# Scores of two heads per matmul: 64x64 array tiles in place of 32x64 ones in a gated mix of linear and sliding-window attention

## The chip, the cores and the metric

The kernel runs on one core of a Trainium2 chip. The metric is the device time of one execution in microseconds. Each kernel is run several times; the median is given. One execution is also profiled.

## The reference

Two attention blocks read the same input x (1 x 2048 x 1024, bf16) and a per-row gate mixes them. Block A is linear attention, block B attends to eight earlier positions at distances 0, 2, ..., 14. Both have 32 heads of 32.

```python
g = sigmoid((x * gate_w).sum(-1, keepdims=True))
return g * A(x, A_wqkv, A_wo) + (1 - g) * B(x, B_wqkv, B_wo)

# A:  pq, pk = phi(q), phi(k);  kv = pk^T v;  z = pk.sum(s)
#     o = (pq @ kv) / (pq . z + 1e-6);  o @ wo
# B:  idx = pos[:, None] - 2 * arange(8)[None, :]          # masked where idx < 0
#     logits = einsum(q[s], k[idx[s, w]]) * 32 ** -0.5
#     o = softmax(logits) @ v[idx];  o @ wo
```

## The kernel before

Rows of x are split by parity into two halves of 1024, so that a window of distance 2 becomes eight neighbouring rows within a half. x is loaded transposed, and the kernel computes V of block B (written to HBM), then K and Q of block B for the first half, then for the second half, then phi(K) of block A, then a matrix mT = xn^T phi(K) and from it the state kv (`state`, L1607), and at last queries, folds and outputs. All these are groups of eight or sixteen matmuls on the full 128x128 array with 512 columns (L1349, L1628, L1700), each into one bank of PSUM; while the windows of block B are worked on, these groups have banks 0 to 3 (0 to 2 later) and the windows have banks 4 to 7 (`SO`).

The windows of block B are done in eighteen *fills*, nine for each half, which are slipped in between those groups (`slot`, one fill in about five groups). Here they are numbered 0 to 17. A fill serves 2 x 57 query rows (2 x 56 in the last of a half), for all heads: two sets of 57 queries, each with its 64 keys. One fill is these steps:

- two DMAs bring the 2 x 64 rows of V back from HBM (tile `v`).
- the **scores burst** (`s_fn`, L1448): for 8 chunks c of four heads, 2 sets h and 4 heads j of a chunk, a matmul of 32 rows (one head's dimensions) by 64 columns (keys) with 57 moving columns (queries). The tile of the array is (32 j, 64 h), so that the eight tiles of a chunk can work at once. Head j of a chunk goes to bank 4 + j.
- ScalarE takes the exponentials of all four banks at once (L1454) into `E`, one of two buffers.
- VectorE multiplies them with the mask (L1457).
- three slots later, the **values burst** (`each`, L1468, 64 matmuls of 64 rows by 32 columns) and within it the sums of the exponentials (L1474, eight matmuls of 456 columns against ones), into the same four banks.
- ScalarE takes the reciprocal of the sums by Ln and Exp (L1483, L1484), VectorE multiplies and writes the result over the queries in `qT` (L1485). After the second of these the banks are free for the next scores burst.

GpSimd makes the masks at the start, and late in the kernel adds up z, the sum of phi(K) over the rows (L1588, L1590; sixteen steps, three after each fill's mask). The cast of z (`zb`, L1570) stands in VectorE's queue between the mask of fill 16 and its L1485.

The order on each engine is not written out: `Prog.schedule` plans it from costs given with each operation and from priorities, in several passes, and the instructions are then emitted per engine in that order, with semaphore waits where data or buffers demand it. An engine works its queue in order.

Of the kernel before, what the change touches and what calls it, by code (L numbers as in the profile page):

```python
# [7 lines left out]
ALU = mybir.AluOpType  # L8
AX = mybir.AxisListType
BF16 = mybir.dt.bfloat16  # L10
# [1109 lines left out]
def build_kernel(nc, A_x, A_wqkv, A_wo, B_x, B_wqkv, B_wo, gate_w, out):  # L1120
# [3 lines left out]
    HS = S // 2  # L1124
# [86 lines left out]
    zb = SB([128, 1024], BF16, "zb")  # L1211
    denr = Ring([SB([128, H], F32, "den%d" % i) for i in range(2)])
    mx4 = SB([128, 3], F32, "mx4")
    mx1 = SB([1, 3], F32, "mx1")
    flag = SB([1, 1], I32, "flag")
    zs = SB([128, 16], F32, "zs")
# [41 lines left out]
    def plan(seen):  # L1258
# [26 lines left out]
            return P.op(eng, fn, cost, reads=reads, writes=writes, prio=-1)  # L1285

        C("pool", lambda e: e.memset(ones[:], 1.0), 0.1, [ones.all()])
        for i, (n, offs) in enumerate(KINDS):
            for h, o in enumerate(offs):
                m = mtmp[h]  # L1290
                b0 = o + 64 * h
                C("pool", lambda e, m=m: e.memset(m[:], 1.0), 0.1, [m.all()])

                C("pool", lambda e, m=m, n=n, b0=b0: e.affine_select(out=m[:, :, 0:n], in_=m[:, :, 0:n], compare_op=ALU.is_ge, fill=0.0, base=b0,
                                                                     pattern=[[0, 2], [1, n]], channel_multiplier=-1), 0.3, [m.all()], [m.all()])
                C("pool", lambda e, m=m, n=n, b0=b0: e.affine_select(out=m[:, :, 0:n], in_=m[:, :, 0:n], compare_op=ALU.is_ge, fill=0.0, base=7 - b0,
                                                                     pattern=[[0, 2], [-1, n]], channel_multiplier=1), 0.3, [m.all()], [m.all()])
                C("dve", lambda e, m=m, n=n, h=h, i=i: e.tensor_copy(msk[i][64 * h:64 * h + 64, :, :], m[64 * h:64 * h + 64, :, 0:n]), 0.2, [msk[i].all()], [m.all()])
                P.ops[-1].prio = 1100
# [132 lines left out]
        masks = []  # L1432
        slot_n = [0]

        def fill(e_, qs, nq, offs):
            t0 = e_ * HS
            k0 = [qs + nq * h - offs[h] for h in range(2)]
# [2 lines left out]
            for h in range(2):  # L1440
                P.op("sp", lambda e, h=h: e.dma_start(vt[64 * h:64 * h + 64, :], vB_hbm[t0 + k0[h]:t0 + k0[h] + 64, :]), 0.4,
                     reads=[hb(t0 + k0[h], t0 + k0[h] + 64, i) for i in range(2)], writes=[vt.all()], chan="v%d_%d" % (vslot, h), lat=0.5)

            def s_fn(e):
                for c in range(8):
                    for h in range(2):
                        for j in range(4):
                            last = e.matmul(SO[j].ap(c * nq, (c + 1) * nq)[64 * h:64 * h + 64, :], kT[32 * j:32 * j + 32, c, t0 + k0[h]:t0 + k0[h] + 64],  # L1448
                                            qT[32 * j:32 * j + 32, c, t0 + qs + h * nq:t0 + qs + (h + 1) * nq], start=True, stop=True, tile_position=(32 * j, 64 * h))
                return last  # L1450
            P.op("pe", s_fn, 0.65, mode="r", reads=[kT.part((0, 8), (t0 + k0[0], t0 + k0[1] + 64)), qT.part((0, 8), (t0 + qs, t0 + qs + 2 * nq))],
                 writes=[s.iv for s in SO], name="S")
            E, _ = Er.next()
            P.op("act", lambda e: e.activation(E[:, 0:32 * nq].rearrange("p (j q) -> p j q", j=4), ps[:, 4:8, 0:8 * nq], ACT.Exp), act(32 * nq),  # L1454
                 reads=[s.iv for s in SO], writes=[E.all()])
# [5 lines left out]
            def values():  # L1461

                def each(e):
                    for c in range(8):
                        for j in range(4):
                            for h in range(2):
                                hd = 4 * c + j
                                last = e.matmul(SO[h].ap(c * nq, (c + 1) * nq)[32 * j:32 * j + 32, :], vt[64 * h:64 * h + 64, hd * 32:hd * 32 + 32],  # L1468
                                         E[64 * h:64 * h + 64, (8 * j + c) * nq:(8 * j + c + 1) * nq],
                                         start=True, stop=True, tile_position=(64 * h, 32 * j))  # L1470
                        if c == SUMS_AT:
                            for j in range(4):
                                for h in range(2):
                                    e.matmul(SO[2 + h].ap(0, 8 * nq)[32 * j:32 * j + 32, :], ones[64 * h:64 * h + 64, 0:32],  # L1474
                                             E[64 * h:64 * h + 64, 8 * j * nq:8 * (j + 1) * nq],
                                             start=True, stop=True, tile_position=(64 * h, 32 * j))
                    return last
                bi = [s.iv for s in SO]
# [347 lines left out]
```

## Time and profile before

| | us |
|---|---|
| median of 3 runs (lowest to highest) | 485.57 (485.45 to 485.61) |
| the profiled execution | 485.35 |
| its span, first to last instruction | 483.5 |
| TensorE busy | 480.0 |
| VectorE, ScalarE, GpSimd busy | 294.9, 146.9, 39.4 |
| granted TensorE clock (share of full) | 1.00 |

In the lines of the profile, PE is TensorE's matmuls and PEld its weight loads, DVE is VectorE, ACT ScalarE, POOL GpSimd. A line of a timeline has the start in us, the length in us, the engine, the line of the kernel, the operation, what it writes and reads, the shapes and the count; merged lines run from the first start to the last end. In brackets stands the idle time before and what ended it. The end of a matmul is modelled: matmuls overlap, so the distance from start to start tells more than the length.

### The profile page before, as it was taken

The numbers are of one execution on the slowest core, as the hardware profiler recorded it, in microseconds if no ns is written. First come the engines' busy times: TensorE is split into PE (matmuls) and PEld (weight loads), VectorE is DVE, ScalarE is ACT, GpSimd is POOL, SyncE is SP. The second block draws the span as 40 slices with busy tenths as digits, with TensorE's granted clock in tenths as the row PEclk, the third lists the DMA queues.
The fourth block names the chain that finished last, engine by engine and source line by source line (L and its number), as shares of the span: only waits on it lengthen the run. The fifth ranks groups of instructions, "written<-read, shape, count | busy, mean of one in ns | idle before, by whom it ended". The sixth has DMA issues, their size and how long they took to land.

```text
span 483.5 us, 10963 instructions
## 1 busy us (share of the span) xinstructions
PE 480.0 (99%) x4882; PEld 229.0 (47%) x4882; DVE 294.9 (61%) x490; ACT 146.9 (30%) x229; POOL 39.4 (8%) x40
## 2 busy tenths in 40 slices
PE   9999999999999999999999999999999999999997
PEld 6444444444444444444455555444444444444444
DVE  2212186799777778766733222489987777767522
ACT  2111111112344446666654356264222000011000
POOL 3000000000000000000015757010000000000000
DMA  8999996223100032013004340571234111122111
GB/s 243 203 190 322 340 342 188 81 94 107 26 23 26 25 110 73 27 34 111 24 25 122 129 104 4 132 197 24 65 89 87 45 43 45 44 66 66 45 45 48
DMA packets 73977, 48.51 MB, mean 100 GB/s; under 512 B 38337, under 2 KB 67394, under 8 KB 73922
## 3 DMA queue, kind: packets, MB, share of 16 engines
q1 hardware_dynamic: 73090, 46.94, 35.5%
q10 hardware_dynamic: 832, 0.79, 0.8%
q8 instruction: 40, 0.66, 0.6%
q14 instruction: 15, 0.12, 0.1%
HBM read 30.41 MB, written 8.39 MB: 80 GB/s over the span
## 4 chain that ended last, share of the span: by engine, by line
PE 99%; DVE 0%; issue 0%
PE ps_all L1349 58%; PE ps_all L1700 23%; PE ps_all L1628 12%; PE ps_all L1448 2%; PE ps_all L1468 2%; PE ps_all L1385 1%; PE ps_all L1474 1%; PE ps_all L1607 1%; PE ps_all L1655 0%; DVE o L1379 0%
## 5 line engine op out<-in xcount | busy, mean ns | idle before, releaser
L1349 PE MATMUL ps_all<-w,xT 128*128 128x512 bf16 x512 | 112.9, 379 | 0.0
L1349 PE MATMUL ps_all<-xT,w 128*128 128x512 bf16 x512 | 112.2, 379 | 0.0
L1349 PEld LDWEIGHTS ps_all<-xT,w 128*128 128x128 bf16 x512 | 49.3, 98 | 58.7
L1349 PEld LDWEIGHTS ps_all<-w,xT 128*128 128x128 bf16 x512 | 49.0, 98 | 57.6
L1355 ACT ACTIVATE e<-ps_all 128x512 bf16<-128x512 f32 x64 | 38.2, 597 | 109.5 <-PE ps_all L1349 108.7
L1700 PE MATMUL ps_all<-w,qT 128*128 128x512 bf16 (+1 forms) x264 | 60.7, 373 | 0.0
L1700 PE MATMUL ps_all<-kT,aT 128*128 128x512 bf16 (+1 forms) x264 | 60.7, 373 | 0.0
L1349 PE MATMUL ps_all<-kT,xT 128*128 128x512 bf16 x256 | 57.9, 379 | 0.0
L1628 PE MATMUL ps_all<-pk,xn 128*128 128x512 bf16 x256 | 57.8, 380 | 0.0
L1700 PEld LDWEIGHTS ps_all<-w,qT 128*128 128x128 bf16 x264 | 25.8, 98 | 29.6 <-issue 0.2
L1700 PEld LDWEIGHTS ps_all<-kT,aT 128*128 128x128 bf16 x264 | 25.8, 98 | 29.4
L1349 PEld LDWEIGHTS ps_all<-kT,xT 128*128 128x128 bf16 x256 | 24.7, 98 | 30.0 <-issue 0.7
L1376 DVE CAST vst<-ps_all 128x512 bf16<-128x512 f32 x16 | 11.1, 692 | 45.4 <-PE ps_all L1349 45.4
L1628 PEld LDWEIGHTS ps_all<-pk,xn 128*128 128x128 bf16 x256 | 23.9, 98 | 27.4
L1379 DVE TENSOR_SCALAR o<-ps_all,gm 128x512 bf16<-128x512 f32 (+1 forms) x27 | 19.7, 731 | 28.0 <-PE ps_all L1700 28.0
L1356 DVE TENSOR_SCALAR e<-e 128x512 bf16<-128x512 bf16 x64 | 18.8, 296 | 27.5 <-ACT e L1355 27.2
L1454 ACT ACTIVATE E<-ps_all 128x1824 bf16<-128x1824 f32 (+1 forms) x18 | 30.4, 1688 | 15.8 <-PE ps_all L1448 15.1
L1457 DVE TENSOR_TENSOR E<-E,msk 128x1824 bf16<-128x1824 bf16 (+1 forms) x18 | 19.8, 1103 | 23.3 <-ACT E L1454 23.3
L1590 POOL TENSOR_TENSOR zacc<-zacc,pk 128x1024 f32<-128x1024 f32 x15 | 32.0, 2130 | 16.5 <-DVE E L1457 15.7
L1485 DVE TENSOR_TENSOR qT<-ps_all,L 128x456 bf16<-128x456 f32 (+1 forms) x36 | 21.2, 625 | 19.4 <-ACT L L1484 19.2
L1377 ACT ACTIVATE kT<-ps_all 128x512 bf16<-128x512 f32 x25 | 14.2, 599 | 33.6 <-PE ps_all L1349 33.6
L1377 ACT ACTIVATE vst<-ps_all 128x512 bf16<-128x512 f32 x16 | 9.6, 597 | 48.7 <-PE ps_all L1349 48.7
(63 smaller groups left out, 361.0 us busy)
## 6 DMA issues: line engine op xcount, KB each, us to landing
v<-vB_hbm SPq DMA_DIRECT2D x36, 128.0 KB, 2.6
vB_hbm<-vst SPq DMA_DIRECT2D x32, 128.0 KB, 4.9
w<-in_B_wqkv_dram SPq DMA_DIRECT2D x4, 1024.0 KB, 8.4
xt<-in_A_x_dram SPq DMA_DIRECT2D x16, 256.0 KB, 5.3
w<-in_A_wqkv_dram SPq DMA_DIRECT2D x4, 1024.0 KB, 9.7
xn<-in_A_x_dram SPq DMA_DIRECT2D x8, 512.0 KB, 3.7
out_dram<-o SPq DMA_DIRECT2D x15, 256.0 KB, 2.1
kT<-in_A_wqkv_dram SPq DMA_DIRECT2D x2, 1024.0 KB, 5.6
```

The lines of the kernel that those rows point to most:

```text
L1349: last = e.matmul(bank.ap(), lhs(dc), rhs(dc), start=(dc == 0), stop=(dc == 7))
L1355: P.op("act", lambda e: e.activation(e_[:, :], bank.ap(), ACT.Exp), act(512), reads=[bank.iv], writes=[e_.all()])
L1356: P.op("dve", lambda e: e.tensor_scalar(e_[:, :], e_[:, :], 1.0, 1e-6, op0=ALU.min, op1=ALU.add), 0.25, reads=[e_.all()], writes=[e_.all()])
L1376: fd = lambda e: e.tensor_copy(dst, src())
L1377: fa = lambda e: e.activation(dst, src(), ACT.Copy)
L1379: fd = lambda e: e.tensor_scalar(dst, src(), scale, None, op0=ALU.mult)
L1454: P.op("act", lambda e: e.activation(E[:, 0:32 * nq].rearrange("p (j q) -> p j q", j=4), ps[:, 4:8, 0:8 * nq], ACT.Exp), act(32 * nq), rea ...
L1457: mk = P.op("dve", lambda e: e.tensor_tensor(ev(), ev(), m[:, :, :].rearrange("p r q -> p (r q)")[:, None, :].to_broadcast([128, 16, 2 * n ...
L1485: P.op("dve", lambda e, L=L, pb=pb, g=g: e.tensor_tensor(qT[:, 4 * g:4 * g + 4, t0 + qs:t0 + qs + 2 * nq].rearrange("p c (h q) -> p h c q" ...
L1590: P.op("pool", lambda e, t=t: e.tensor_tensor(zacc[:, :], zacc[:, :], pkS[:, t, :], ALU.add), 2.2, reads=[src, zacc.all()], writes=[zacc.a ...
L1628: last = e.matmul(bank.ap(), tl[:, t, cs:cs + 128], pkS[:, t, r * 512:(r + 1) * 512], start=(t == 0), stop=(t == NT - 1))
L1700: last = e.matmul(bank.ap(0, f1 - f0), lh[:, k, t * 128:(t + 1) * 128], w[:, k, f0:f1], start=(first and k == 0), stop=(not first and k == 7))
```

## The change

The scores burst takes two heads at a time. A matmul now has 64 rows, the dimensions of two heads, on one of four 64x64 tiles of the array, and 114 moving columns: 57 queries with head 0's dimensions and zeros in head 1's rows, then the same 57 queries with the zeros in head 0's rows. A burst has 32 matmuls in place of 64. The moving operand is a new tile `qx`, filled by two GpSimd multiplications per fill with a column of `pick` (ones in the rows of every other head, zeros elsewhere). The pair for the next fill is issued right after the scores burst of the present one, and the burst waits for it. `qx` lies where the second exponentials buffer was; `E` has one buffer. The scores lie in another order in the four banks and in `E`, so the reads of the values and sums change their offsets; the sums read `E` in eight runs of 57 in place of 456 in a row. In the built program, the order on TensorE changes in one place: at the end of the phase the last values burst stands ahead of the first eight matmuls of the queries and apart from the last state burst.

```diff
+    pick = SB([128, 2], F32, "pick")
...
-    Er = Ring([SB([128, 32 * 57], BF16, "E%d" % i) for i in range(2)])
+    Er = Ring([SB([128, 32 * 57], BF16, "E")])
+    qx = SB([128, 8 * 4 * 57], BF16, "qx")
...
+        C("dve", lambda e: e.memset(pick[:, :], 0.0), 0.1, [pick.all()])
+        P.ops[-1].prio = 1100
+        for i in range(4):
+            C("dve", lambda e, i=i: e.memset(pick[32 * i:32 * i + 32, i % 2:i % 2 + 1], 1.0), 0.1, [pick.all()], [pick.all()])
+            P.ops[-1].prio = 1100
...
+        ready = []
+
+        def spread(e_, qs, nq, offs):
+            ready.append((e_, qs))
+            for i in range(2):
+                P.op("pool", lambda e, i=i: e.tensor_scalar(qx[:, 0:32 * nq].rearrange("p (c h s q) -> p c h s q", c=8, h=2, s=2)[:, :, :, i, :],
+                                                            qT[:, :, e_ * HS + qs:e_ * HS + qs + 2 * nq].rearrange("p c (h q) -> p c h q", h=2), pick[:, i:i + 1], None, op0=ALU.mult),
+                     0.9, reads=[pick.all(), qT.part((0, 8), (e_ * HS + qs, e_ * HS + qs + 2 * nq))], writes=[qx.all()])
...
+            if (e_, qs) not in ready:
+                spread(e_, qs, nq, offs)
 
             def s_fn(e):
                 for c in range(8):
                     for h in range(2):
-                        for j in range(4):
-                            last = e.matmul(SO[j].ap(c * nq, (c + 1) * nq)[64 * h:64 * h + 64, :], kT[32 * j:32 * j + 32, c, t0 + k0[h]:t0 + k0[h] + 64],
-                                            qT[32 * j:32 * j + 32, c, t0 + qs + h * nq:t0 + qs + (h + 1) * nq], start=True, stop=True, tile_position=(32 * j, 64 * h))
+                        for g in range(2):
+                            last = e.matmul(SO[2 * g + c // 4].ap(c % 4 * 2 * nq, (c % 4 + 1) * 2 * nq)[64 * h:64 * h + 64, :], kT[64 * g:64 * g + 64, c, t0 + k0[h]:t0 + k0[h] + 64],
+                                            qx[64 * g:64 * g + 64, (2 * c + h) * 2 * nq:(2 * c + h + 1) * 2 * nq], start=True, stop=True, tile_position=(64 * g, 64 * h))
                 return last
...
+            if todo:
+                spread(*todo[0])
...
-                                         E[64 * h:64 * h + 64, (8 * j + c) * nq:(8 * j + c + 1) * nq],
+                                         E[64 * h:64 * h + 64, (j // 2 * 16 + 2 * c + j % 2) * nq:(j // 2 * 16 + 2 * c + j % 2 + 1) * nq],
...
                                     e.matmul(SO[2 + h].ap(0, 8 * nq)[32 * j:32 * j + 32, :], ones[64 * h:64 * h + 64, 0:32],
-                                             E[64 * h:64 * h + 64, 8 * j * nq:8 * (j + 1) * nq],
+                                             E[64 * h:64 * h + 64, j // 2 * 16 * nq:(j // 2 + 1) * 16 * nq].rearrange("p (c s q) -> p c s q", c=8, s=2)[:, :, j % 2, :],
```

More of the change, by code (lines that the diff above doesn't have):

```diff
@@ L1446, in s_fn @@
                     for h in range(2):
-                        for j in range(4):
-                            last = e.matmul(SO[j].ap(c * nq, (c + 1) * nq)[64 * h:64 * h + 64, :], kT[32 * j:32 * j + 32, c, t0 + k0[h]:t0 + k0[h] + 64],
-                                            qT[32 * j:32 * j + 32, c, t0 + qs + h * nq:t0 + qs + (h + 1) * nq], start=True, stop=True, tile_position=(32 * j, 64 * h))
-                return last
-            P.op("pe", s_fn, 0.65, mode="r", reads=[kT.part((0, 8), (t0 + k0[0], t0 + k0[1] + 64)), qT.part((0, 8), (t0 + qs, t0 + qs + 2 * nq))],
-                 writes=[s.iv for s in SO], name="S")
+                        for g in range(2):
+                            last = e.matmul(SO[2 * g + c // 4].ap(c % 4 * 2 * nq, (c % 4 + 1) * 2 * nq)[64 * h:64 * h + 64, :], kT[64 * g:64 * g + 64, c, t0 + k0[h]:t0 + k0[h] + 64],
+                                            qx[64 * g:64 * g + 64, (2 * c + h) * 2 * nq:(2 * c + h + 1) * 2 * nq], start=True, stop=True, tile_position=(64 * g, 64 * h))
+                return last
+            P.op("pe", s_fn, 0.6, mode="r", reads=[kT.part((0, 8), (t0 + k0[0], t0 + k0[1] + 64)), qx.all()], writes=[s.iv for s in SO], name="S")
+            if todo:
+                spread(*todo[0])
             E, _ = Er.next()
```

## The prediction

> **What bounds the kernel now.** I read the page first (busy time, chain of waits), then the timeline of one scores burst, then its lines by source, then the GpSimd rows and the stretch in which GpSimd works.
>
> ```profile
> PE 480.0 (99%) x4882; PEld 229.0 (47%) x4882; DVE 294.9 (61%) x490; ACT 146.9 (30%) x229; POOL 39.4 (8%) x40
> PE 99%; DVE 0%; issue 0%
> ```
>
> TensorE is busy from end to end and the chain of waits runs on it alone: nothing makes it wait. So the time is the sum of TensorE's work, and a step counts if it shortens a stretch of TensorE or makes TensorE wait for the first time. The profiled run took 485.35 us, 483.5 of it span; the median of the runs is 485.57, 0.22 more, which I add at the end.
>
> **The scores burst, now.** Eighteen bursts (1152 matmuls, 64 each). The first, in the timeline:
>
> ```profile
> 124.94 0.38 PE L1349 MATMUL ps_all<-xT,w 128*128 128x512 bf16 x1
> 125.25 0.33 PE L1448 MATMUL ps_all<-qT,kT 32*64 32x57 bf16 x32
> 125.25 0.70 PE L1448 MATMUL ps_all<-qT,kT 32*64 32x57 bf16 x64
> 125.88 0.39 PE L1349 MATMUL ps_all<-xT,w 128*128 128x512 bf16 x1
> ...
> L1448 PE MATMUL ps_all<-qT,kT x32: 182/207/208, 125.5 to 125.7; 32*64 32x57 bf16 x32
> L1448 PE MATMUL ps_all<-qT,kT x1152: 181/207/211, 125.2 to 306.2; 32*64 32x57 bf16 x172, 32*64 32x56 bf16 x20
> ```
>
> (The second row is the stretch up to 125.40, the third the whole burst; the fifth counts the second half alone.) From the full-array matmul before it to the one after it, 125.88 - 124.94 = 0.94 us. That is 0.31 until the first scores matmul starts; the burst; and 0.14 from the last start (125.95 less its 0.207 = 125.74) to the next full-array matmul. The burst falls in two. Of the first 32 the row ends at 125.58; less one matmul of some 0.19, the last of them starts at 125.39, so 32 matmuls start within 0.14 us: four rounds over the eight 32x64 tiles, 0.035 a round. The other 32 start from 125.48 to 125.74, 0.26 us for the same work. The second half goes at the pace at which instructions arrive (0.26/32 = 8 ns a pair), the first at the pace of the array. A burst of 32 in all goes through without the step, which the state burst shows:
>
> ```profile
> 258.64:258.68 0.04, 0.03 (x4) 0.03 (x8) 1.00 0.00 0
> 258.68:258.71 0.03, 0.03 (x8) 0.03 (x12) 1.00 0.00 0
> ...
> 258.83:258.86 0.03, 0.03 (x32) 0.03 (x15) 1.00 0.00 0
> ```
>
> (Stretches of L1607 alone; the first x counts its matmuls started so far.) Four more every 25 ns, all 32 within 0.20 us.
>
> **The burst after.** 32 matmuls of 114 columns on four tiles: eight rounds, at the array's pace. What a column costs is in the sums, 456 columns on eight tiles at once:
>
> ```profile
> 131.44 0.19 PE ps_all L1474 x8
> ```
>
> 0.19/456 = 0.42 ns a column; 114 take 0.0475. Each round I take at 0.050: 0.0025 more for the step from one matmul to the next, as the full-array ones start 0.215 apart (worked out below) for 512 x 0.42 = 0.2125. First to last start are 7 x 0.050 + 0.012 = 0.362, the 0.012 for the last round's four starts (0.14/32 = 0.004 apart, as in the first half); the way in stays 0.31; the way out is 0.14 plus the 0.024 by which the last matmul is longer. Sum 0.836, 0.104 less than 0.94; times 18, **1.87 us less**. Bounds: no extra per round gives 0.82, 2.2 us less; the 0.011 by which a round of the first half exceeds its 0.024 gives 0.89, 1.0 us less. I take a value near the better end, as 0.035 is a mean that has the first filling of the tiles in it.
>
> **The end of the phase.** The built program's order on TensorE is the same but for one place: the last values burst moves ahead of 8 matmuls and no longer stands directly before the last state burst.
>
> ```profile
> 308.70 1.24 PE L1628 MATMUL ps_all<-pk,xn 128*128 128x512 bf16 x5
> 309.87 0.38 PE L1607 MATMUL ps_all<-mT,w 128*32 128x32 bf16 x32
> ...
> 314.02 0.50 PE L1468 MATMUL ps_all<-E,v 64*32 64x56 bf16 x40
> 314.46 0.37 PE L1607 MATMUL ps_all<-mT,w 128*32 128x32 bf16 x32
> ```
>
> Alone, a state burst starts 0.31 after the last full-array matmul (five of them, the modelled 0.38 long: (1.24 - 0.38)/4 = 0.215 apart, the last at 309.56); behind the values it starts 0.13 after their last (314.52 - 0.19 = 314.33). **0.19 more, once.** Its copy to kvT, of 256 columns, then has 16 matmuls (3.4 us) before the fold in place of 24; that hides it, since the cast of 1024 further down takes 0.69. The values' mask now goes ahead of a reduction on VectorE, so it is early enough.
>
> **GpSimd and what it blocks.** Each fill gains two multiplications of 912 elements; the first pair has five groups of eight matmuls (8 us) before it is needed, each later one starts when the scores burst before it ends. The trace has none. Nearest rows:
>
> ```profile
> L1588 POOL CAST zacc<-pk 128x1024 f32<-128x1024 bf16 x1 | 1.0, 1037 | 246.0 <-DVE E L1457 246.0
> L1580 POOL COPY zb<-zr 128x1024 bf16<-128x1024 bf16 x1 | 2.0, 2032 | 18.7 <-DMA zr<-z_hbm 18.7
> L1590 POOL TENSOR_TENSOR zacc<-zacc,pk 128x1024 f32<-128x1024 f32 x15 | 32.0, 2130 | 16.5 <-DVE E L1457 15.7
> ```
>
> By elements: 0.92 us from the cast, 1.81 from the copy (which reads with a stride of eight), 1.90 from the two-input add. I take 0.95, by the cast: one input, unit stride. A pair is 2 x 0.95 + 0.08 = 2 us.
>
> ```profile
> 319.69 2.03 POOL L1580 COPY zb<-zr 128x1024 bf16<-128x1024 bf16 x1 [18.71 <-DMA zr<-z_hbm]
> 321.20 0.68 DVE L1356 TENSOR_SCALAR e<-e 128x512 bf16<-128x512 bf16 x1
> L1356 DVE TENSOR_SCALAR e<-e x64: 272/294/681, 184.3 to 447.0; 128x512 bf16<-128x512 bf16 x64
> ```
>
> L1356 takes 0.29, but 0.68 under the copy, and it ends 0.16 after the copy does: it was held until GpSimd was done. The mask (L1457) also reads and writes SBUF alone, so I take it as held too. The Trainium skill (SBUF — State Buffer, Who interferes with whom) says so outright: a VectorE instruction with two SBUF inputs and a GpSimd one that reads SBUF share a port, and the later one waits; no trace here shows the mask under GpSimd work.
>
> What that costs, in a fill of the middle and in the stretch where GpSimd also adds up z:
>
> ```profile
> 197.56 0.29 DVE L1356 TENSOR_SCALAR e<-e 128x512 bf16<-128x512 bf16 x1 [0.61 <-ACT e L1355]
> 199.31 1.11 DVE L1457 TENSOR_TENSOR E<-E,msk 128x1824 bf16<-128x1824 bf16 x1 [0.74 <-ACT E L1454]
> 201.01 0.28 PE L1468 MATMUL ps_all<-E,v 64*32 64x57 bf16 x23
> ...
> 286.39 0.70 PE L1448 MATMUL ps_all<-qT,kT 32*64 32x57 bf16 x64
> 288.89 1.11 DVE L1457 TENSOR_TENSOR E<-E,msk 128x1824 bf16<-128x1824 bf16 x1 [3.54 <-ACT E L1454]
> 290.08 6.54 POOL L1590 TENSOR_TENSOR zacc<-zacc,pk 128x1024 f32<-128x1024 f32 x3 [2.23 <-DVE E L1457]
> 290.58 0.28 PE L1468 MATMUL ps_all<-E,v 64*32 64x57 bf16 x24
> 292.95 1.17 DVE L1485 TENSOR_TENSOR qT<-ps_all,L 128x456 bf16<-128x456 f32 x2 [2.96 <-ACT L L1484]
> 295.17 0.70 PE L1448 MATMUL ps_all<-qT,kT 32*64 32x57 bf16 x64
> 297.67 1.11 DVE L1457 TENSOR_TENSOR E<-E,msk 128x1824 bf16<-128x1824 bf16 x1 [3.54 <-ACT E L1454]
> 298.86 2.13 POOL L1590 TENSOR_TENSOR zacc<-zacc,pk 128x1024 f32<-128x1024 f32 x1 [2.24 <-DVE E L1457]
> 301.02 0.69 DVE L1570 CAST zb<-zacc 128x1024 bf16<-128x1024 f32 x1 [2.24 <-POOL zacc L1590]
> 303.42 0.63 DVE L1485 TENSOR_TENSOR qT<-ps_all,L 128x456 bf16<-128x456 f32 x1
> 305.68 0.70 PE L1448 MATMUL ps_all<-qT,kT 32*64 32x56 bf16 x64
> ```
>
> Scores, mask, values: the mask ends 0.58 before the values burst (290.58 - 290.00). In fills 6 to 10 (first rows) the pair comes behind an L1356 that ends at 197.85: first half to 198.80, second to 199.83; the mask, ready at 199.31, is held until then and ends 0.96 later (1.11 - 0.15, as L1356), at 200.79; the values are due at 201.01: nothing lost, 0.2 to spare. In the z stretch GpSimd's load per fill becomes 6.54 + 2.0 = 8.5 of the 8.78 us between bursts, and the adds wait for the mask, which waits for the pair. TensorE comes 0.1 earlier with each fill after 11 (the last before which GpSimd is idle), GpSimd does not. The adds of fill 14 end at 287.9 as now (290.08 - 2.23). Then: first half of the pair to 288.9; mask, ready at 288.5, from there to 289.8 (values due at 290.58 - 0.4 = 290.2); second half to 290.8; adds of fill 15 to 297.4; mask of fill 16, ready at 297.2, held by them, to 298.4 (values due 298.8); last pair to 300.3; last add 300.4 to 302.5, which is 1.5 later than in its row. The cast to zb waits for it in VectorE's queue, and behind the cast stands the eviction L1485, which ends at 305.6 instead of 304.05. The last scores burst would by then come at 305.68 - 0.6 = 305.1 and needs that eviction's banks: with 0.1 for the signal, **0.6 us of waiting**.
>
> Off the path: the one E buffer, since E's next exponentials read banks that the scores write only after the values burst has read E; five small memsets at the start, before any work needs VectorE; the sums' read of E in runs of 57, taken at 0.19 as now (the values read such runs already).
>
> **Sum:** -1.87 + 0.19 + 0.6 = -1.08: 485.35 becomes 484.27, with 0.22 on it **484.5**.
>
> **Rivals.** (1) The mask is not held: GpSimd then keeps its pace, the last add ends no later than now, and the 0.6 goes: -1.68, **483.9**. For it: two L1485, with one input in PSUM, take 1.17 under the adds, no longer than the 0.63 of one alone; against it: L1356's 0.68.
>
> (2) On the other side: GpSimd's multiplication is slower than the cast suggests, and the held mask makes the values burst wait. Place: fills 6 to 10, with 0.2 to spare at 0.95. At 1.3 us each the second half ends at 197.85 + 2.68 = 200.53, the mask at 201.49, the values are late by 0.55 with the signal: 2.8 us in five fills, 0.3 in fill 11, and some 1.5 at the last burst for the later adds: 4.6 - 1.7 = +2.9, **488.5**. It decides from about 1.1 us a multiplication. For it: the copy and the add, both above 1.8; against: the cast.
>
> (3) Weights no longer load under the matmul that runs. With eight tiles there is always another tile to work; with four, load and matmul of one tile could stand in line: 0.0475 + 0.0275 a round (the 64 columns by 0.42 ns, and 1 ns), 7 x 0.075 + 0.012 = 0.54, burst 1.01, +0.07 x 18 + 0.19 = +1.5, **487.0**. Against it: in the first half a round of 0.035 holds a load of 0.027 and a matmul of 0.024, 0.051 in line. A rule for it is in the Trainium skill (TensorE: Matmul & The Clock Gate, The mechanism): a weight load overlaps running matmuls only where the row group differs, and there are two groups now for four. By that rule as written the 0.035 would not be possible either.
>
> (4) The change does not do what it says: the burst keeps 0.94. Then +0.19 and up to 0.6 for GpSimd, **486.1**. Against it: the state burst's even 25 ns.
>
> **How the numbers follow.** Forecast 0.42, (1) 0.15, (2) 0.27, (3) 0.09, (4) 0.07. The forecast's own range: 1.0 to 2.2 for the bursts and 0 to 1.2 for the wait, 483.6 to 486.0. The range 483.4 to 488.6 takes in (1) with the better bound, (3), (4) and the milder half of (2). A measurement of this kernel can tell 0.2%, 1 us: faster is below 484.6, where half of the forecast and nearly all of (1) lie, 0.24 + 0.14 = 0.38. Slower is above 486.5: (2) 0.22, (3) 0.08, (4) and the forecast's edge 0.05, 0.35. The rest, 0.27.
>
> **What would show it.** Right: scores bursts of about 0.84 from full-array matmul to full-array matmul, eight even rounds of 0.05; GpSimd multiplications of 0.95; masks longer than 1.11 behind them; TensorE idle only before the last scores burst. Wrong: rounds of 0.075; TensorE idle before values bursts; a multiplication over 1.1; masks at 1.11 with GpSimd busy.

## The result, and the profile after

The changed kernel takes 501.0 us (median of 6 runs, 499.57 to 501.29) against 485.59 (6 runs, 485.42 to 486.30) before: ratio 1.0308, 95% interval 1.0298 to 1.0319. It is 3.1% slower, far above the forecast of 484.5 and above the top of its range, 488.6.

The profiled execution took 499.57 us, span 497.8. The first row of the page and the chain of waits, after:

```profile
PE 474.4 (95%) x4241; PEld 227.5 (46%) x4306; DVE 305.5 (61%) x495; ACT 146.3 (29%) x229; POOL 143.7 (29%) x76
...
PE 84%; POOL 13%; issue 1%; DVE 1%
```

TensorE has less work than before (474.4 for 480.0; some 60 matmul records are missing, so the difference is not exact) but no longer runs through, and GpSimd, 39.4 us busy before, stands at 143.7 and on the chain. The scores burst of fill 0 in the timeline:

```profile
124.96 0.38 PE L1356 MATMUL ps_all<-xT,w 128*128 128x512 bf16 x1
125.27 0.60 PE L1466 MATMUL ps_all<-qx,kT 64*64 64x114 bf16 x32
125.80 0.39 PE L1356 MATMUL ps_all<-xT,w 128*128 128x512 bf16 x1
```

From full-array matmul to full-array matmul it takes 125.80 - 124.96 = 0.84 us, as forecast, for 0.94 before. GpSimd's multiplication by source (durations in ns, lowest, median, highest):

```profile
L1447 POOL TENSOR_SCALAR qx<-qT,pick x36: 2523/2602/4024, 115.9 to 310.7; 128x912 bf16<-128x912 bf16 x32, 128x896 bf16<-128x896 bf16 x4
```

It takes 2.60 us in the median in place of the 0.95 assumed; all 36 together, 102.5. TensorE's waits (us in total, times, longest):

```profile
PE ps_all L1466 <- POOL qx L1447: 5.3, 2, 2.6
PE ps_all L1466 <- DVE qT L1504: 5.2, 1, 5.2
...
PE ps_all L1487 <- DVE E L1476: 1.8, 2, 1.0
```

Scores bursts now wait for the multiplication and for an eviction, values bursts for a mask. How this comes about in the stretch where GpSimd also adds up z (L1609), in the timeline:

```profile
283.12 5.24 POOL L1447 TENSOR_SCALAR qx<-qT,pick 128x912 bf16<-128x912 bf16 x2
...
288.32 7.28 POOL L1609 TENSOR_TENSOR zacc<-zacc,pk 128x1024 f32<-128x1024 f32 x3
...
288.50 0.59 PE L1466 MATMUL ps_all<-qx,kT 64*64 64x114 bf16 x32 [2.63 <-POOL qx L1447]
...
290.87 2.74 DVE L1476 TENSOR_TENSOR E<-E,msk 128x1824 bf16<-128x1824 bf16 x1 [6.11 <-ACT E L1473]
...
293.67 0.28 PE L1487 MATMUL ps_all<-E,v 64*32 64x57 bf16 x24 [1.01 <-DVE E L1476]
...
295.59 5.24 POOL L1447 TENSOR_SCALAR qx<-qT,pick 128x912 bf16<-128x912 bf16 x2
...
300.98 0.97 PE L1466 MATMUL ps_all<-qx,kT 64*64 64x114 bf16 x32 [2.63 <-POOL qx L1447]
...
308.05 5.14 POOL L1447 TENSOR_SCALAR qx<-qT,pick 128x896 bf16<-128x896 bf16 x2
...
313.16 2.12 POOL L1609 TENSOR_TENSOR zacc<-zacc,pk 128x1024 f32<-128x1024 f32 x1
315.31 0.69 DVE L1589 CAST zb<-zacc 128x1024 bf16<-128x1024 f32 x1 [9.22 <-POOL zacc L1609]
...
317.59 0.62 DVE L1504 TENSOR_TENSOR qT<-ps_all,L 128x456 bf16<-128x456 f32 x1
...
318.27 0.96 PE L1466 MATMUL ps_all<-qx,kT 64*64 64x112 bf16 x32 [5.20 <-DVE qT L1504]
```

GpSimd is never idle here. One round, a pair and three adds, lasts 5.24 + 7.28 = 12.5 us (283.12 to 295.59), where 8.8 us lay between bursts before. TensorE now runs at GpSimd's pace: scores wait for their pair, values for a mask that was held under the adds (2.74 us for 1.11), and the last scores burst for the chain that the prediction had named: last z add, cast to zb, second eviction L1504. The waits are 5.3 + 5.2 + 1.8 = 12.3 us. The granted clock adds to them (a stretch, its length, busy us of PE, weight loads, DVE, ACT, POOL; then the clock, the share of the DMA engines and GB/s):

```profile
284.00:301.00 17.00, 10.52 (x179) 5.12 (x180) 4.67 (x5) 5.44 (x9) 16.66 (x8) 1.00 0.03 9
301.02:304.42 3.40, 3.18 (x38) 1.61 (x39) 0.70 (x1) 1.69 (x1) 3.32 (x2) 0.50 0.02 5
...
318.10:321.50 3.40, 2.90 (x37) 1.64 (x39) 0.12 (x1) 1.66 (x1) 0.00 (x0) 0.50 0.70 160
```

Behind two of the waits TensorE has half its clock for 3.4 us, some 1.7 us lost each time (an estimate: half of 3.4, TensorE being busy for 3.18 and 2.90 of it). So 12.3 + 3.4 + 0.2 (the last values burst, no longer ahead of a state burst) - 1.9 (the bursts) = 14.0; the spans differ by 497.8 - 483.5 = 14.3. The profiled execution is the quickest of the six and has a mean granted clock of 0.993, where the others have 0.986 to 0.993, so that the median of 501.0 may hold more of the lost clock than this sum.

### The profile page after: what moved, and what is told of

Read it like the earlier page. It is cut to its first block, busy times and chain, and to the rows that moved or that the text cites. A ratio compares the mean times of both kernels' runs of the same rounds, so it can differ in the third digit from the quotient of the medians.

```text
span 497.8 us, 9798 instructions
## 1 busy us (share of the span) xinstructions
PE 474.4 (95%) x4241; PEld 227.5 (46%) x4306; DVE 305.5 (61%) x495; ACT 146.3 (29%) x229; POOL 143.7 (29%) x76
## 4 chain that ended last, share of the span: by engine, by line
PE 84%; POOL 13%; issue 1%; DVE 1%
PE ps_all L1356 55%; PE ps_all L1719 22%; POOL zacc L1609 7%; POOL qx L1447 6%; PE ps_all L1647 2%; PE ps_all L1466 1%; PE ps_all L1487 1%; PE ps_all L1392 1%; PE ps_all L1493 0%; PE ps_all L1674 0%; DVE zlo L1590 0%; DVE qT L1504 0%; POOL zacc L1607 0%; DVE zb L1589 0%; PE ps_all L1626 0%
## 5 line engine op out<-in xcount | busy, mean ns | idle before, releaser
L1447 POOL TENSOR_SCALAR qx<-qT,pick 128x912 bf16<-128x912 bf16 (+1 forms) x36 | 102.5, 2848 | 171.4 <-DVE qT L1386 110.1
L1356 PE MATMUL ps_all<-w,xT 128*128 128x512 bf16 x493 | 109.5, 379 | 2.6 <-issue 2.3
L1356 PE MATMUL ps_all<-xT,w 128*128 128x512 bf16 x497 | 110.1, 379 | 1.6 <-issue 1.3
L1356 PEld LDWEIGHTS ps_all<-xT,w 128*128 128x128 bf16 x512 | 49.4, 98 | 58.9
L1356 PEld LDWEIGHTS ps_all<-w,xT 128*128 128x128 bf16 x512 | 48.9, 98 | 58.1 <-issue 0.2
L1356 PE MATMUL ps_all<-kT,xT 128*128 128x512 bf16 x253 | 57.4, 379 | 0.4 <-issue 0.3
L1476 DVE TENSOR_TENSOR E<-E,msk 128x1824 bf16<-128x1824 bf16 (+1 forms) x18 | 25.0, 1388 | 27.4 <-ACT E L1473 27.4
L1356 PEld LDWEIGHTS ps_all<-kT,xT 128*128 128x128 bf16 x256 | 24.6, 98 | 29.8 <-issue 0.7
L1363 DVE TENSOR_SCALAR e<-e 128x512 bf16<-128x512 bf16 x64 | 20.2, 316 | 25.7 <-ACT e L1362 25.6
L1609 POOL TENSOR_TENSOR zacc<-zacc,pk 128x1024 f32<-128x1024 f32 x15 | 34.1, 2275 | 0.8
L1504 DVE TENSOR_TENSOR qT<-ps_all,L 128x456 bf16<-128x456 f32 (+1 forms) x36 | 21.1, 624 | 19.5 <-ACT L L1503 19.5
L1315 DVE TENSOR_TENSOR mx<-mx,qT 128x1024 bf16<-128x1024 bf16 x32 | 23.6, 772 | 1.3 <-ACT qT L1387 1.2
```

What stands on the lines that cost most here:

```text
L1315: P.op("dve", lambda e, m=m, op=op: e.tensor_tensor(m[:, 0:n], m[:, 0:n], src, op), 0.08 + n / 1920.0, reads=[m.all(), reg], writes=[m.all()],
L1356: last = e.matmul(bank.ap(), lhs(dc), rhs(dc), start=(dc == 0), stop=(dc == 7))
L1363: P.op("dve", lambda e: e.tensor_scalar(e_[:, :], e_[:, :], 1.0, 1e-6, op0=ALU.min, op1=ALU.add), 0.25, reads=[e_.all()], writes=[e_.all()])
L1447: P.op("pool", lambda e, i=i: e.tensor_scalar(qx[:, 0:32 * nq].rearrange("p (c h s q) -> p c h s q", c=8, h=2, s=2)[:, :, :, i, :], qT[:, ...
L1476: mk = P.op("dve", lambda e: e.tensor_tensor(ev(), ev(), m[:, :, :].rearrange("p r q -> p (r q)")[:, None, :].to_broadcast([128, 16, 2 * n ...
L1504: P.op("dve", lambda e, L=L, pb=pb, g=g: e.tensor_tensor(qT[:, 4 * g:4 * g + 4, t0 + qs:t0 + qs + 2 * nq].rearrange("p c (h q) -> p h c q" ...
```

## The experiments

Theory A: GpSimd's time alone makes the loss; the multiplication takes 2.6 us, and together with the z adds it fills GpSimd beyond the time there is. The rivals blame the new bursts or the one E buffer (B), the waiting for qx at each burst (C), the place of the spread in any engine's queue (D), or the holding of VectorE (G, H).

**The bursts alone.** One pair of multiplications in place of eighteen.

```diff
-            for i in range(2):
+            for i in range(2 if len(ready) == 1 else 0):
```

> This kernel is the changed one with only the first pair of GpSimd multiplications: qx is filled once, and the scores of the later fills are worked out from the first fill's queries (that part of the output is other data). Scores bursts, layout of E, the single E buffer are those of the change. Theory A (the loss is GpSimd's multiplication, 2.6 us for 0.95): TensorE no longer waits, the scores bursts keep their saving of 0.104 us each, 18 of them, 1.87 less; the last values burst goes back to the place that it has before the change, so that the 0.19 falls away: 483.7 us, 0.4% faster than before, PE idle under 0.5 us in all, no stretch at half clock. Rival B (the new bursts, their order or the one E buffer cost time themselves): still some 495 to 501, with TensorE idle or at half clock.

Measured: 484.5 us (5 runs, 483.70 to 484.71; before 485.86), ratio 0.9962 [0.9949, 0.9976]: 1.8 us less by the ratio (1.2 to 2.5 by its interval, 1.4 by the medians), 1.87 forecast for the bursts. The order of work on TensorE is that of the kernel before. TensorE's waits are one row, at the start, which every kernel here has:

```profile
PE ps_all L1392 <- PEq L1830: 0.8, 1, 0.8
```

B falls: bursts, layout and the single E buffer are a gain, of the size that was predicted.

**The multiplications alone.** The kernel before, with the pairs written to a tile nobody reads, and with one E buffer. TensorE's order is that of the change.

```diff
+            if todo:
+                spread(*todo[0], past=[sc])
```

(`sc` is the scores burst of 64 matmuls; the multiplications are as in the change.)

> This kernel is the one before with the 36 GpSimd multiplications added (and one E buffer): they write a tile that nobody reads, each pair starts when the scores burst ahead of it has ended, and the scores bursts are the old ones with 64 matmuls. Theory A: the multiplications alone make the loss. TensorE no longer waits for qx, but each fill in the stretch of the z adds needs 2 x 2.6 + 6.5 = 11.7 us of GpSimd where 8.8 lie between the bursts, five fills, so that the last z add ends 10 to 14 us late, the cast to zb with it, and behind that the eviction that the last scores burst waits for: 495 to 500 us, one wait of about 10 us in place of several. Rival C (what costs is the wait of TensorE for qx at each burst, the GpSimd time itself finds room): 485 to 487. Rival B: 485.6, as before.

Measured: 501.17 us (4 runs, 500.52 to 501.64), ratio 1.0311 [1.0294, 1.0327], the whole loss with none of the new bursts. Now nobody waits for qx, and the backlog comes out in one place, the chain behind the last z add:

```profile
313.88 2.12 POOL L1610 TENSOR_TENSOR zacc<-zacc,pk 128x1024 f32<-128x1024 f32 x1
316.03 0.69 DVE L1590 CAST zb<-zacc 128x1024 bf16<-128x1024 f32 x1 [16.59 <-POOL zacc L1610]
...
319.00 0.79 PE L1466 MATMUL ps_all<-qT,kT 32*64 32x56 bf16 x64 [12.58 <-DVE qT L1505]
```

12.6 us in one wait, a little more than expected; 0.6 more stands before a values burst, and the granted clock was at half for 13.7 us, 5.4 of them behind the long wait. C falls as the main cause: 15.3 us are lost although nobody waits for qx. The change loses 15.4 after a gain of 1.7 from its bursts, so up to some 2 us of its loss are not in this run.

**GpSimd's forms by themselves**, in the first 80 us of the kernel before.

```diff
+            "ptr_runs": lambda e: e.tensor_scalar(o_(), r_(fi, n_), fp[:, 0:1], None, op0=ALU.mult),
+            "ptr": lambda e: e.tensor_scalar(fo[:, 0:n_], fi[:, 0:n_], fp[:, 0:1], None, op0=ALU.mult),
+            "imm": lambda e: e.tensor_scalar(fo[:, 0:n_], fi[:, 0:n_], 1.0, None, op0=ALU.mult),
+            "copy_runs": lambda e: e.tensor_copy(o_(), r_(fi, n_)),
+            "tt": lambda e: e.tensor_tensor(fo[:, 0:n_], fi[:, 0:n_], fi[:, 0:n_], ALU.mult),
...
```

> The kernel before, with GpSimd operations on scratch data put into the first 80 us, in which GpSimd has nothing to do: each form twice alone, then four of them beside a VectorE instruction (two inputs like the mask, 912 elements; then one input of 512 like the clamp of phi). The time of the whole kernel is not what is read here. Forms: multiplication by a column of scalars with the output in runs of 57 (as in the change), the same unbroken, the same with 456 elements, by a constant, a copy in runs and unbroken, a product of two inputs, an f32 add, the copy with a stride of eight. Theory E: the kind of operation sets the price; a multiplication by a column of scalars takes 2.6 us for 912 elements, in runs or not, 1.3 for 456, and a copy 0.95 to 1.0. Theory F: the layout sets it: unbroken 0.95, in runs of 57 2.6, for the multiplication and the copy alike. On holding: by the prediction VectorE's instruction waits for the GpSimd one in all pairs; by the trace of the changed kernel only beside the two-input add, and beside the multiplication not.

The groups of GpSimd's instructions (busy us, mean ns), in the stretch where they stand alone; L1312 is the form of the change, L1313 the same unbroken, L1315 by a constant, L1314 half as long, L1316 a copy in runs and L1317 unbroken, L1318 a product of two inputs:

```profile
L1312 POOL TENSOR_SCALAR fo<-fi,fp 128x912 bf16<-128x912 bf16 x2 | 5.2, 2591 | 0.2
L1313 POOL TENSOR_SCALAR fo<-fi,fp 128x912 bf16<-128x912 bf16 x2 | 5.1, 2566 | 0.2
L1315 POOL TENSOR_SCALAR fo<-fi 128x912 bf16<-128x912 bf16 x2 | 5.0, 2490 | 0.2
...
L1318 POOL TENSOR_TENSOR fo<-fi 128x912 bf16<-128x912 bf16 x2 | 3.4, 1707 | 0.2
L1314 POOL TENSOR_SCALAR fo<-fi,fp 128x456 bf16<-128x456 bf16 x2 | 2.9, 1426 | 0.2
...
L1316 POOL COPY fo<-fi 128x912 bf16<-128x912 bf16 x2 | 1.9, 967 | 0.1
L1317 POOL COPY fo<-fi 128x912 bf16<-128x912 bf16 x2 | 1.9, 949 | 0.1
```

The kind of operation sets the price (theory E), not the layout: runs of 57 cost 0.02 us. The copy takes what the prediction took for the multiplication; the multiplication by one scalar per partition takes 2.7 times that, more than a product of two whole inputs. From 456 to 912 elements it grows by 1.14 us: 2.5 ns an element and some 0.3 besides. Of the pairs beside VectorE, in the same run, two:

```profile
43.96 2.59 POOL L1312 TENSOR_SCALAR fo<-fi,fp 128x912 bf16<-128x912 bf16 x1 [0.18 <-POOL fo L1312]
...
44.81 0.66 DVE L1327 TENSOR_TENSOR fd<-fd,fi 128x912 bf16<-128x912 bf16 x1
...
54.17 2.01 POOL L1320 COPY fo<-fi 128x1024 bf16<-128x1024 bf16 x1
...
55.17 1.51 DVE L1327 TENSOR_TENSOR fd<-fd,fi 128x912 bf16<-128x912 bf16 x1
```

At its quickest VectorE's instruction takes 0.64. Under the copy (here the one of 1024 elements with a stride of eight; under the plain copy it took 1.43) it ends 0.5 after the copy, held; under the multiplication it runs through. (Another one under a multiplication took 1.23, yet ended 1.07 before it: delayed, not held to the end. The f32 add was itself delayed beside VectorE, 1.61 for 1.15.)

**The z adds earlier**, the multiplication left as it is: one add for every two tiles of phi(K) as they are ready.

```diff
                 slot(FILL)
+                if r and t % 2 == 0 and t:
+                    z_add(1)
```

The cost of a multiplication given to the planner is 2.6 here in place of 0.9.

> The changed kernel with GpSimd's multiplication of 2.6 us kept, and the z adds begun earlier: one for every two tiles of k features as these are ready, while the fills before the z stretch run, in which GpSimd stands idle for 4.7 of 10.1 us a fill; the rest where they were. Nothing else is changed. Theory A: it is GpSimd's time in the z stretch that counts, not the multiplication as such. GpSimd has then 16 x 2.13 + 11 x 5.3 = 92 us of work from the first k tile to the last scores burst, some 105 us: it fits, if barely: 484 to 486. Rival G (the multiplication costs by holding VectorE's mask or by its place ahead of each burst): 495 to 500 as with the change. Rival H (moved adds hold the masks of earlier fills, in which they then stand): waits of TensorE before values bursts, 487 to 490.

Measured: 483.97 us (4 runs, 483.59 to 484.42; before 486.12), ratio 0.9955 [0.9939, 0.9970]: faster than both kernels. The multiplications are no shorter, as GpSimd's row shows, but TensorE waits for nothing beside the row at the start, as with the bursts alone:

```profile
L1447 POOL TENSOR_SCALAR qx<-qT,pick 128x912 bf16<-128x912 bf16 (+1 forms) x36 | 104.3, 2896 | 162.7 <-DVE qT L1386 110.5 <-PE ps_all L1466 50.9
```

So 104 us of slow multiplications cost nothing where GpSimd has the time. G and H fall for this form. With the new cost and the earlier adds the planned order moved in several places on TensorE as well, and the new cost with late adds was not run, so this run does not tell the two apart. The last experiment below keeps every order.

**A quicker form: the product of two inputs** (1.71 us), with the z adds late as in the change, and then with an early add for every tile. The cost of a product given to the planner is 1.7 here in place of 0.9.

```diff
-                P.op("pool", lambda e, i=i: e.tensor_scalar(qx[:, 0:32 * nq].rearrange("p (c h s q) -> p c h s q", c=8, h=2, s=2)[:, :, :, i, :],
-                                                            qT[:, :, e_ * HS + qs:e_ * HS + qs + 2 * nq].rearrange("p c (h q) -> p c h q", h=2), pick[:, i:i + 1], None, op0=ALU.mult),
+                P.op("pool", lambda e, i=i: e.tensor_tensor(qx[:, 0:32 * nq].rearrange("p (c h s q) -> p c h s q", c=8, h=2, s=2)[:, :, :, i, :],
+                                                            qT[:, :, e_ * HS + qs:e_ * HS + qs + 2 * nq].rearrange("p c (h q) -> p c h q", h=2), pick[:, i:i + 1, None, None].to_broadcast([128, 8, 2, nq]), ALU.mult),
```

> The changed kernel with the spread on GpSimd as a product of two inputs, the queries and a column of bf16 zeros and ones broadcast along them, in place of the multiplication by a column of scalars: measured alone 1.71 us for 2.59. The z adds stay where they are. Theory A (GpSimd has too little time in the stretch of the z adds): a pair takes 3.5 us in place of 5.3, GpSimd's load per fill there 10.0 of 8.8 in place of 11.9, so five or six fills run up 6 to 7 us less its slack: of the 12.6 us by which the last scores burst is late with the slow multiplication and the old bursts, 5.5 x 1.76 = 9.7 go: some 3 us of waiting are left, 1.7 gained by the bursts: 486 to 488. Rival G (holding: a two-input product shares the port with the mask and the max of VectorE, which the multiplication by scalars does not): masks of 2 us and more in all fills, TensorE waits before values bursts: 490 and over.

> Both of the two: the two-input product (1.71 us) and a z add for each tile of k features as it is ready. GpSimd's load is 16 x 2.13 + 11 x 3.5 = 73 of 105 us. Theory A: no wait of TensorE on GpSimd is left: 483.7 to 484.1 us, 0.3 to 0.4% faster than before, as the bursts alone gave. Rival H (two-input work of GpSimd against the masks and the max of VectorE, now in every fill): masks of 2 us, waits before values bursts, 486 to 489.

Measured: 496.06 us (4 runs, 495.48 to 496.58), ratio 1.0201 [1.0185, 1.0216], and with the early adds 491.75 (4 runs, 491.19 to 492.23), ratio 1.0112 [1.0097, 1.0128]. Both misses. The wait that GpSimd's time had made did shrink, in the first from 5.3 for qx to 0.5, and in the second 0.4 is left, for an eviction before the scores burst of fill 13; but in its place stands another, here fill 6 of the first in the timeline:

```profile
199.64 3.50 POOL L1447 TENSOR_TENSOR qx<-qT,pick 128x912 bf16<-128x912 bf16 x2 [8.33 <-PE ps_all L1466]
199.69 1.81 DVE L1363 TENSOR_SCALAR e<-e 128x512 bf16<-128x512 bf16 x1 [0.61 <-ACT e L1362]
...
202.14 1.96 DVE L1476 TENSOR_TENSOR E<-E,msk 128x1824 bf16<-128x1824 bf16 x1
...
204.16 0.28 PE L1487 MATMUL ps_all<-E,v 64*32 64x57 bf16 x24 [1.05 <-DVE E L1476]
```

and TensorE's waits for masks in the second:

```profile
PE ps_all L1487 <- DVE E L1476: 6.8, 6, 1.6
```

Each half of the pair holds VectorE until it ends (the clamp in phi, L1363, L1356 before the change: 1.81 us for 0.29; the mask 1.96 for 1.10), and the values burst is late: in fill 0, and in fills 6 to 10, the place that rival 2 had named (in the first kernel 0.4 more stands late in the z stretch). Up to there the order on TensorE is that of the change. In the second kernel 6.8 + 0.4 - 1.9 = 5.3 us, where the profiled execution (492.23) lies 6.1 above the median before. In the first, 7.3 before values bursts, 0.5 before a scores burst and 2.8 after the last fill, less 1.9, make 8.7 of the 10.5 by which its profiled execution (496.58) lies above; the rest I have not placed. From the last fills on, the planned order is another in both: in the first the cast of z stands behind the second eviction, so that the last scores burst does not wait for the last z add, and the 2.8 may belong to the new order.

**The spread on VectorE**, for the last six fills only, then for all.

```diff
-                P.op("pool", lambda e, i=i: e.tensor_scalar(qx[:, 0:32 * nq].rearrange("p (c h s q) -> p c h s q", c=8, h=2, s=2)[:, :, :, i, :],
+                P.op("pool" if e_ == 0 or qs < 2 * 57 * 3 else "dve", lambda e, i=i: e.tensor_scalar(qx[:, 0:32 * nq].rearrange("p (c h s q) -> p c h s q", c=8, h=2, s=2)[:, :, :, i, :],
```

For all eighteen the engine is "dve" throughout; the planner's cost on VectorE is 0.5.

> The changed kernel with the pairs of the last six fills (those that share GpSimd with the z adds) on VectorE, at 0.5 us each, and the first twelve on GpSimd as in the change, 2.6 us. TensorE's order of work is that of the kernel with the bursts alone. Theory A: GpSimd's slow multiplication is hidden where GpSimd has no other work, and the z adds keep the pace they had: 483.7 to 484.2. Rival G (the multiplication costs through VectorE's work in every fill): over 485.5. Rival D (the spread on VectorE costs by its place in VectorE's queue, as all eighteen on VectorE gave 489.9): 486 to 488, with waits of TensorE for VectorE after the last fills.

> The changed kernel with the same two multiplications a fill on VectorE (cost given to the planner 0.5 us). VectorE has a multiplication of the same kind, 128x512 bf16 in 0.29 us; for 912 elements by that 0.5 us, 36 of them 18 us of an engine that is busy for 305 of 498. Theory A: GpSimd is free again, the adds keep their pace, and the bursts' saving stays: 483.9 us (1.87 less, 0.19 more at the last values burst if it stays apart), multiplications 0.4 to 0.6 us. Rival B: 495 to 501, since the bursts are the same. Rival D (a spread ahead of each burst costs on any engine, because it stands in the queue of an engine that TensorE needs): 485 to 488, with waits of TensorE for VectorE ahead of the values or scores bursts.

Measured: the last six 484.21 us (5 runs, 483.96 to 484.42), ratio 0.9961 [0.9948, 0.9975]; all eighteen 489.92 (5 runs, 488.61 to 490.91), ratio 1.0087 [1.0073, 1.0102], against theory A. The multiplication took 0.51 us there in the mean, and no scores burst waited for it; the waits lay behind the last values burst, 4.4 us in five rows, the longest of them

```profile
PE ps_all L1719 <- DVE p L1365: 1.5, 1, 1.5
```

At a cost of 0.5 the planner had put several values bursts behind eight more matmuls, and the last state burst ahead of the last values burst. With 0.2 in place of 0.5 as its cost, and nothing else changed, it keeps the order that TensorE has with the last six on VectorE.

> All eighteen pairs on VectorE, as in the run that gave 489.9, but with a cost of 0.2 us given to the planner for each in place of 0.5, with which TensorE's order is word for word that of the kernel with the last six pairs on VectorE (values bursts not moved behind eight more matmuls, last state burst and folds in their old places). It tells apart what the 4 us of the former run were. Theory A (the order that the planner chose at 0.5): 483.7 to 484.3, no wait after the last fill. Rival D (18 us more of work in VectorE's queue): 487 to 490, with waits for VectorE before values bursts or evictions.

Measured: 484.25 us (9 runs, 483.64 to 484.85; before 485.53), ratio 0.9970 [0.9960, 0.9980]. The 18 us of multiplications on VectorE cost nothing; the 4 us came with the planned order. D falls.

**The price as predicted.** A plain copy on GpSimd in place of the multiplication, every order as in the change.

```diff
-                P.op("pool", lambda e, i=i: e.tensor_scalar(qx[:, 0:32 * nq].rearrange("p (c h s q) -> p c h s q", c=8, h=2, s=2)[:, :, :, i, :],
-                                                            qT[:, :, e_ * HS + qs:e_ * HS + qs + 2 * nq].rearrange("p c (h q) -> p c h q", h=2), pick[:, i:i + 1], None, op0=ALU.mult),
+                P.op("pool", lambda e, i=i: e.tensor_copy(qx[:, 0:32 * nq].rearrange("p (c h s q) -> p c h s q", c=8, h=2, s=2)[:, :, :, i, :],
+                                                            qT[:, :, e_ * HS + qs:e_ * HS + qs + 2 * nq].rearrange("p c (h q) -> p c h q", h=2)),
```

> The changed kernel with a plain copy on GpSimd in place of each multiplication, which took 0.97 us alone in runs of 57, about the 0.95 of the prediction. (What is left out is the setting to zero: qx then holds the queries of both heads in all rows, and the scores of a fill are other data.) All orders are those of the change. It tests what of the prediction stands once the one price is as assumed. Theory A (only the price was wrong): the prediction's sum, 1.87 less, 0.19 more at the last values burst, 0 to 0.6 of waiting for the chain of the last z add: 483.9 to 484.5 us; masks of fills 6 to 10 held to about 2 us by the copy, but the values burst not late, as there is 0.2 to spare. Rival 2 of the prediction, by holding instead of by price: the two-input product of 1.71 us held the masks of fills 6 to 10 and TensorE waited 1.1 each; if the copy and VectorE's work hold each other (alone, a copy took 1.44 beside a two-input instruction) a pair takes up to 2.9 us, and the values burst of fills 6 to 10 is late by up to 0.7: up to 3.5 us more, 485 to 488.

Measured: 484.13 us (7 runs, 483.64 to 484.87), ratio 0.9969 [0.9958, 0.9980], that is 1.5 us less; 1.1 less was forecast. GpSimd's copies by group:

```profile
L1447 POOL COPY qx<-qT 128x912 bf16<-128x912 bf16 x32 | 32.7, 1023 | 211.8 <-DVE qT L1386 110.4 <-PE ps_all L1466 100.4
```

Fill 7, in which the pair holds the clamp (1.02 us for 0.29) and the mask loses only 0.07 (some 0.9 was expected), and the end, where the last add and the scores burst behind it are in time:

```profile
207.33 1.93 POOL L1447 COPY qx<-qT 128x896 bf16<-128x896 bf16 x2 [8.12 <-PE ps_all L1466]
207.39 1.02 DVE L1363 TENSOR_SCALAR e<-e 128x512 bf16<-128x512 bf16 x1 [0.70 <-ACT e L1362]
...
209.05 1.17 DVE L1476 TENSOR_TENSOR E<-E,msk 128x1824 bf16<-128x1824 bf16 x1
...
298.59 2.13 POOL L1609 TENSOR_TENSOR zacc<-zacc,pk 128x1024 f32<-128x1024 f32 x1
...
304.29 0.59 PE L1466 MATMUL ps_all<-qx,kT 64*64 64x112 bf16 x32
```

This kernel and the changed one differ in one GpSimd instruction, with the order on TensorE, VectorE and ScalarE the same in both traces, and by 16.9 us. Rival 2 by holding did not come about at this length.

## Why the prediction was wrong, point by point

- **The scores burst.** Its total is right, 0.838 against 0.836, and eighteen of them gave 1.8 us by the ratio in the kernel with the bursts alone; that the total came so close is luck. From first to last start it takes 0.389 in place of 0.362: the second round of four starts 0.074 after the first, the later ones some 0.05 apart. The way out takes 0.140 in place of 0.164: it did not grow with the longer matmul, and no run shows why. The two errors cancel. The worse bound was also added up wrongly: with 0.011 more a round the burst is 0.896, a gain of 0.8 us and not 1.0. That the second half of the old burst goes at the pace of arriving instructions is not shown; the runs show that a burst of 32 has no such second half. Rivals 3 (weights no longer load under the matmul) and 4 (the burst stays) are out.
- **GpSimd's multiplication, 0.95 us.** This step failed; everything else follows from it. It was priced by the cast of one input at unit stride, with 1.9 as the highest of the rows quoted; it takes 2.6, and with a copy of 0.95 to 0.97 in its place, all else as it was, the kernel takes 484.13. The reasoning by inputs and strides was wrong: the copy fits it (0.97), the multiplication by scalars is a form of its own, and none of the rows quoted bounded it.
- **The bounds were not carried through.** The text had the sum that matters, 6.54 + 2.0 = 8.5 of 8.78 us of GpSimd per fill, and did not ask what happens past 8.78, that is past 1.1 us a multiplication. At 1.9, the highest row that it quoted, a pair takes 3.9 and the load is 10.4, a backlog of 1.6 us in each of about five fills (an estimate by its own sum). Rival 2 stopped at 1.3 us and worked out the values bursts, with 1.5 us at the last scores burst for later adds, so that 488.6 was no top. It put the turn at about 1.1 us, which by this load is right, for another reason.
- **The mask is held by the multiplication.** Not seen: in fills 6 to 10 of the changed kernel masks take 1.11 and values bursts do not wait, although the pair runs past them, fill 7 for one:

```profile
207.04 5.36 POOL L1447 TENSOR_SCALAR qx<-qT,pick 128x896 bf16<-128x896 bf16 x2 [4.69 <-PE ps_all L1466]
207.07 0.29 DVE L1363 TENSOR_SCALAR e<-e 128x512 bf16<-128x512 bf16 x1 [0.71 <-ACT e L1362]
...
208.70 1.11 DVE L1476 TENSOR_TENSOR E<-E,msk 128x1824 bf16<-128x1824 bf16 x1 [0.61 <-ACT E L1473]
```

  It holds for two-input products (1.96), and, between mask and z adds, in the changed kernel itself (2.74). The Trainium skill (SBUF — State Buffer, Who interferes with whom) says that a VectorE instruction with two SBUF inputs and a GpSimd one that reads SBUF exclude each other for the whole instruction; the runs agree for GpSimd's copies and two-input forms, and not for its multiplication by scalars, beside which masks took 1.11 and the product on VectorE 0.66 for 0.64 at its quickest. The two do not leave each other quite alone, though: in the changed kernel VectorE's running maximum and minimum (tile `mx`, two inputs) took up to 1.43 for 0.68 under the multiplication, one mask of the kernel with the early adds 1.48, and the multiplication 3.74 for 2.59 in the pairs for fills 1 to 5; what decides it stays open.
- **The wait of the last scores burst.** The chain was right, last add, cast, eviction; its size was not, 5.2 us for 0.6, since the adds ended 12.8 us later than forecast (315.28 for 302.5). At the forecast price the last add ended at 300.7, and the 0.6 went.
- **The last values burst, 0.19** (by the figures quoted, 0.31 - 0.13 = 0.18). Right as far as a trace tells. In the kernel with the price as predicted, whose order is that of the change, the state burst starts 314.78 - (314.85 - 0.38) = 0.31 after the last full-array matmul:

```profile
311.45 3.40 PE L1356 MATMUL ps_all<-kT,xT 128*128 128x512 bf16 x15 [0.16 <-issue]
314.78 0.38 PE L1626 MATMUL ps_all<-mT,w 128*32 128x32 bf16 x32
```

With the bursts alone, in the old order, it starts 313.66 - (313.74 - 0.19) = 0.11 after the last values matmul:

```profile
313.23 0.51 PE L1487 MATMUL ps_all<-E,v 64*32 64x56 bf16 x40
313.66 0.38 PE L1626 MATMUL ps_all<-mT,w 128*32 128x32 bf16 x32
```

- **The clock** was no term of the sum: two stretches at half clock cost some 3.4 us together.
- **The one E buffer** and the sums' read in runs cost nothing, as said.

## What to carry to other kernels

Price an operation by a row of the same kind on the same engine, not by its elements, inputs and strides; where the trace has no such row, the bound is open at the top, and the range has to show what happens once it is passed. Work handed to an idle engine is free only in the stretches in which that engine is idle: add up its load stretch by stretch against the time between the events that need it, and if it does not fit, move its other work (here the z adds, begun earlier) before giving up the gain. A shorter instruction is not always the better one: at 1.71 us the two-input form held VectorE, and its kernel lost 5.6 us with an early z add for every tile, where the one of 2.6 us cost nothing with an early add for every second tile.

## What the runs showed of the hardware

- GpSimd, 912 bf16 elements a partition: copy 0.95, product of two inputs 1.71, multiplication by a scalar column 2.57, by a constant 2.49; output in runs of 57 adds 0.02.
- The same multiplication on VectorE takes 0.46 us in most cases, up to 1.04, and 0.50 to 0.51 in the mean.
- After a wait of 2.6 us TensorE ran at half clock for 3.4 us once (301.0) and not the other time (288.5); the waits of 1.0 to 1.6 us in the two-input kernels were followed by none. The Trainium skill (TensorE: Matmul & The Clock Gate, What's actually happening) puts the fall to half speed after an idle window of about 3.4 us; here a shorter wait sufficed once. The changes of the clock lie 3.41 us or a multiple of it apart: at 301.01, 304.43, 318.08 and 321.50 in the changed kernel, at 310.75 and 324.41 with the multiplications alone. If the clock is decided in such steps, an estimate from these times, the wait with half clock behind it lies within one step (297.6 to 301.0), and the other is cut in two at 287.4; no run tests this.
- 32 matmuls on four 64x64 tiles need no more than 64 on eight 32x64 ones: 0.84 for 0.94 us, way in and out included; the rounds of the four-tile burst start some 0.05 us apart, but for a first step of 0.074.
